# The first layer's sixteen units in groups of 2, 4, 5 and 5, with a new order string and a new table

## The chip, the core and the metric

The kernel runs on one core of one Trainium2 chip. A core has five engines with an instruction queue of their own: TensorE (PE, matmuls; the load of a matmul's weights is listed as PEld), VectorE (DVE), ScalarE (ACT), GpSimd (POOL) and SyncE (SP, which here only issues DMAs). The metric is device time in microseconds of one execution, median over runs.

## The reference

Attention over two batches of eight heads, whose queries are averaged in pairs first, then two feed-forward layers on the result (1152 tokens of 512 values):

```python
q_pool = q.reshape(B, H, S // 2, 2, D).mean(axis=3)          # S = 1152, D = 64
attn   = softmax(q_pool @ k.T / sqrt(D));  x = attn @ v       # -> 1152 x 512
h = x @ w_in                                                  # 512 -> 2048
P = a0 + a1*h + a2*h**2 + a3*h**3
Q = 1 + abs(b0)*abs(h) + abs(b1)*h**2
x = (P / (Q + 1e-6)) @ w_out                                  # 2048 -> 512
xn = x / sqrt(mean(x*x) + 1e-6) * rms_g
y = (silu(xn @ w_gate) * (xn @ w_val)) @ w_out2               # 512 -> 1536 -> 512
```

## The kernel before

All matmuls of the two layers work on float32 split in two halves (hi and lo), and each product is the sum of three matmuls: hi by hi, hi by lo, lo by hi (`three`, whose instruction is line 597 for both layers).

**Attention.** 72 score tiles of 128 query rows by 1152 keys. For each, PE makes the scores into a PSUM tile (hid, line 929), DVE takes the negated maximum of each row (nm, line 961), ACT the exponential (p, line 967), PE transposes p in blocks of 64 (line 983), and ACT or DVE copies the result to pt (lines 1016 and 1019). The matmuls with v (av, line 1088) follow. Copies of the transposed keys and queries (kT, qT, lines 695 and 698), copies of av (xt), and the sums of query pairs (qp, line 765) can go to more than one engine.

**Weights.** Meanwhile the weights of the layers are loaded (wraw, line 165), converted and split (wc, then win or wout, hi and lo; hi on line 200 or 202, lo on line 207). The first ones stay in SBUF; the others of layer 1 are written to DRAM as two halves and fetched again later by two DMAs of 256 KB each, hi and lo (line 247). There are three buffers for the win pairs and six for the wout pairs (`RB, CB, WIN, WOUT = 3, 2, 3, 6`). A fetch can start when PE has read the buffer's former weights for the last time.

**Layer 1.** The 2048 hidden values are 16 units of 128. For each unit PE makes hid (36 matmuls: three chunks of 384 tokens, four pieces of the 512 inputs, three products), then a chain of six DVE and six ACT operations makes g, ending with g_hi on ACT (line 1338) and g_lo on GpSimd or DVE (line 1341). Seven buffers hold g. The units are taken in groups: for each of nine tiles of 128 tokens, PE adds up the products of the group's units in one of two PSUM buffers (accp, 128x512, three matmuls a unit). The first group's result is copied to acc by ACT (line 1390), that of each later group is added to acc by DVE (line 1392).

**Change of layers.** After the last group each tile's squares are summed (ACT, line 1419), three tiles make a chunk of 384 tokens, whose factor is worked out on small tiles (lines 1425 to 1436), the tiles are scaled (line 1442 or 1444), PE transposes them block by block into the same two accp buffers (line 1449, three transposes a block, four blocks a chunk), and ACT and DVE write x_hi (line 1452) and x_lo (line 1455). A table of activation functions is loaded once in between (line 1611).

**Layer 2.** Twelve units of a gate and a value projection (hid again), a tanh on ACT (line 1503), products on DVE (lines 1507 and 1529), and sums over groups of 4, 4, 2 and 2 units (`GROUPS2`); adds on DVE (line 1572), and the output's DMAs.

**What sets the order.** The program is not written in the order in which it runs. Every step is an `Op` with an engine, a cost, a key and its inputs and buffers; the function `order` makes a plan of the whole, step by step, and issues each engine's instructions in the plan's order. The key of a step is moved by one symbol of the string SHIFTS (250 a symbol), and WAYS says for a step that may go to several engines which one it takes (a digit), or leaves it to the plan (a dot). In the attention the sequence on PE is fixed by PE_ORDER: A and C for the scores, T and 2 for the transposes of p, V for av, P for the key and query transposes. Which engine waits for what on the chip is set by semaphores.

Of the kernel before, what the change touches and what calls it, by code (L numbers as in the profile page):

```python
# [19 lines left out]
def attention_moe_moe2_kernel(  # L20
# [94 lines left out]
    GROUPS1 = [2, 4, 4, 4, 2]  # L115
# [159 lines left out]
    def weight(w, u):  # L275
# [13 lines left out]
        "_DIPUPVKN[QDSOU[TWPRLVT@7QPPDMPk`PUUP2T(fbNEHTNPPPWTPKx=KMPm_GPR=PPORKPmWPTOXW=XNPPP<ZPVUNPOPO]`GN@I"  # L289
        "dOC:(PPGVuM<SHP)Q?P-bX@PPCPPPP6Q-ZP?@ZL@TV=P9PM<KQP7PUPpUPPQ]PmNYPPP,SISjPPIPESX(eVe]UcPQSHPPHPYJBIL"  # L290
        "OrPHHOPIKlMRLRJNc@PJOZPdIRHMNTPPPPZPpPPMPY]ORXLWXF?JNPR0PqJSRKPYPWPHP]PYyLRQPD<KFK[(LPULKJNOPFPOQ]PV"
        "]PQ=UZ9PZMWIeORaBQVP`N1PPSGCaPPP;PR]I`>/aTPQG5PPYP_GOM?yGPDTLYPANPWIKR@QPAPBWN+PPH>LX[Od_HQO[PiQ^VPM"
        "LMOMeR=KSCPLP`PPSLPSEMETbUPPPNYPOWJP=fZPTxNTYPCPRQXTPRcPPQCdMOSPKWUPHPURUPTUP>PXTPFCPPPJPPP6Zd_CZAP="
        "KPPPyPAPWLZTPNPPIPP:NYKOKWS9T]P5P;<UmPrPaNLIPPIPZBHeSSLFBPP]RWND<DRaPPT<k`E<YMNMITDGnPDMPKV;7EI0NL]B"
        "QPMPRMbSPLPaRMMOPDYORJP@PP><PQPTPPPKPZOGYyQORDP<PdPMRT?EPMT[ZTPFTKVKPVLRPT?MUP;PPR]IXCPQOrJRT(Ma]PPP"
        "2PVGDVKtJE^KSKYXFPyGRPNMSkULcbGEOPPPPUNQAa^pPoPLCVDDRDT5GGVPVsPLyP5:P]WZQLQLYP:FCQ9HWF>XRd2APPPSPPL9"
# [1356 lines left out]
```

## Time and profile before

| | us |
|---|---|
| median of three runs (690.06, 691.29, 691.69) | 691.29 |
| the profiled execution | 690.4 |
| its span, first to last instruction | 688.6 |
| PE busy in it | 672.0 |
| DVE busy | 539.2 |
| ACT busy | 400.5 |
| POOL busy | 213.7 |

The attention fills the span to about 248 us, layer 1 the time to about 455 us, layer 2 the rest. A matmul's record is longer than the distance to the next one, since matmuls overlap: PE's rows with 0.33 or 0.39 us follow each other at 0.17 and 0.23 us. "Idle before" an instruction is time in which its engine did nothing, and the name behind the arrow is what ended it.

### The profile page before, as it was taken

To read this page: it belongs to the slowest core of one execution; us is meant where nothing else is said; L and a number is where in the kernel's file an instruction comes from. 1 tells how busy PE (TensorE), PEld (TensorE's weight loads), DVE (VectorE), ACT (ScalarE), POOL (GpSimd) and SP (SyncE) were. 2 spreads that over 40 slices of the span, in tenths; PEclk is the share of its full clock that TensorE was granted. 3 is DMA by queue.
4 is the path that set the end of the run, shared out by engine and by line. 5 is a ranking of instruction groups with operands and counts; after the bars stand their busy time and mean duration, and the time that the engine had idled before them with its cause. 6 is when DMAs were issued, how large, how long until landed. Compare 5 with 4: busy or idle time off the path is not lost.

```text
span 688.6 us, 13171 instructions
## 1 busy us (share of the span) xinstructions
PE 672.0 (98%) x5302; PEld 572.0 (83%) x5302; DVE 539.2 (78%) x700; ACT 400.5 (58%) x652; POOL 213.7 (31%) x224
## 2 busy tenths in 40 slices
PE   7999999999999999999999999999999999999997
PEld 6667666776677678999889988889998899989996
DVE  5899998888989858998998999675775245965554
ACT  4777778888889948997568647183343223312130
POOL 3334246656655562111010412012232014421020
PEclk9999999999999999999999999999999999999999
DMA  7544436666546425241032003101225112431003
GB/s 216 187 135 113 124 104 212 200 193 209 207 162 213 166 85 184 91 153 62 32 121 94 31 30 124 62 0 54 101 93 152 31 39 85 126 119 34 28 1 138
DMA packets 54061, 77.67 MB, mean 113 GB/s; under 512 B 6512, under 2 KB 36464, under 8 KB 54000
## 3 DMA queue, kind: packets, MB, share of 16 engines
q1 hardware_dynamic: 53712, 76.50, 34.4%
q8 instruction: 42, 0.69, 0.4%
q10 hardware_dynamic: 288, 0.33, 0.1%
q14 instruction: 19, 0.16, 0.1%
HBM read 62.40 MB, written 14.42 MB: 112 GB/s over the span
## 4 chain that ended last, share of the span: by engine, by line
PE 86%; DVE 7%; ACT 4%; issue 1%; DMA 1%; POOL 0%; SPq 0%; DVEq 0%; ACTq 0%; POOLq 0%
PE hid L597 35%; PE accp L597 25%; PE hid L929 9%; PE av L1088 8%; PE hid L983 7%; DVE nm L961 3%; ACT p L967 3%; DVE pt L1019 1%; PE hid L838 1%; PE accp L1449 1%; DMA qn<-in_q_dram 1%; PE prep L1135 1%; PE prep L838 1%; DVE acc L1572 0%; DVE m_p L1299 0%
## 5 line engine op out<-in xcount | busy, mean ns | idle before, releaser
L597 PE MATMUL hid<-x_hi,win_hi 128*128 128x384 f32 x480 | 161.8, 337 | 1.3 <-DVE m_p L1299 1.3
L597 PE MATMUL hid<-x_hi,win_lo 128*128 128x384 f32 x480 | 160.8, 335 | 0.0
L597 PE MATMUL hid<-x_lo,win_hi 128*128 128x384 f32 x480 | 155.3, 335 | 0.0
L967 ACT ACTIVATE p<-hid,nm 128x1152 f32<-128x1152 f32 x72 | 88.0, 1222 | 32.9 <-DVE nm L961 30.3
L961 DVE TENSOR_REDUCE nm<-hid 128x1 f32<-128x1152 f32 x72 | 96.9, 1356 | 10.3 <-PE hid L929 4.9
L597 PE MATMUL accp<-wout_hi,g_lo 128*128 128x512 f32 (+1 forms) x254 | 99.2, 390 | 0.0
L597 PE MATMUL accp<-wout_lo,g_hi 128*128 128x512 f32 (+1 forms) x254 | 99.0, 390 | 0.0
L597 PE MATMUL accp<-wout_hi,g_hi 128*128 128x512 f32 (+1 forms) x254 | 98.5, 388 | 0.1
L597 PEld LDWEIGHTS hid<-x_hi,win_hi 128*128 128x128 f32 x480 | 90.1, 188 | 4.6 <-issue 2.2
L929 PE MATMUL hid<-kT,qT 64*128 64x256 f32 (+3 forms) x800 | 91.7, 370 | 0.9 <-ACT qT L695 0.5
L597 PEld LDWEIGHTS hid<-x_lo,win_hi 128*128 128x128 f32 x480 | 89.5, 188 | 1.8
L597 PEld LDWEIGHTS hid<-x_hi,win_lo 128*128 128x128 f32 x480 | 90.1, 188 | 0.0
L983 PEld LDWEIGHTS hid<-ident,p 64*128 64x128 f32 x1296 | 51.8, 139 | 38.4 <-ACT p L967 25.0
L1088 PE MATMUL av<-pt,vn 128*64 128x288 f32 x576 | 83.5, 417 | 0.0
L929 PEld LDWEIGHTS hid<-kT,qT 64*128 64x128 f32 (+1 forms) x800 | 72.3, 177 | 11.2 <-issue 1.0
L983 PE MATMUL hid<-ident,p 64*128 64x64 f32 x1296 | 65.3, 229 | 7.5 <-ACT p L967 5.9
L1016 ACT ACTIVATE pt<-hid 128x512 f32<-128x512 f32 (+2 forms) x143 | 59.1, 442 | 12.5 <-PE hid L983 11.0
L1341 POOL TENSOR_TENSOR g_lo<-m_p,g_hi 128x1152 fp32r<-128x1152 f32 (+1 forms) x11 | 22.8, 2084 | 121.9 <-ACT g_hi L1338 84.3
L174 ACT ACTIVATE wc<-wraw 128x512 f32<-128x512 f32 x68 | 45.9, 675 | 24.8 <-POOL win_lo L207 12.0
L1019 DVE COPY pt<-hid 128x512 f32<-128x512 f32 (+2 forms) x81 | 49.9, 621 | 11.0 <-PE hid L983 7.9
L597 PEld LDWEIGHTS accp<-wout_hi,g_lo 128*128 128x128 f32 x254 | 47.7, 188 | 9.9
L597 PEld LDWEIGHTS accp<-wout_hi,g_hi 128*128 128x128 f32 x254 | 47.7, 188 | 8.7 <-DVE acc L1572 0.3
(122 smaller groups left out, 1034.4 us busy)
## 6 DMA issues: line engine op xcount, KB each, us to landing
wraw<-in_moe_w_out_dram SPq DMA_DIRECT2D x28, 512.0 KB, 3.5
far<-spill SPq DMA_DIRECT2D x23, 512.0 KB, 3.2
wraw<-in_moe_w_in_dram SPq DMA_DIRECT2D x16, 512.0 KB, 4.2
wraw<-in_moe_w_gate_dram SPq DMA_DIRECT2D x12, 512.0 KB, 3.8
wraw<-in_moe_w_val_dram SPq DMA_DIRECT2D x12, 512.0 KB, 3.6
vn<-in_v_dram SPq DMA_DIRECT2D x16, 288.0 KB, 3.0
kn<-in_k_dram SPq DMA_DIRECT2D x15, 288.0 KB, 4.4
qn<-in_q_dram SPq DMA_DIRECT2D x15, 256.0 KB, 3.7
```

The lines of the kernel that those rows point to most:

```text
L174: nc.scalar.activation(c.bitcast(F32), wt["raw", n][:, :, 1].bitcast(F32), AF.Abs, scale=2.0**-112)
L597: ins = nc.tensor.matmul(dst, lhsT=a[x], rhs=b[y], start=first and i == 0 and p == 0, stop=last and i == n - 1 and p == len(by) - 1,)
L838: ins = nc.tensor.transpose(e["prep", n_][r][:, at // 2:at // 2 + 64], src[rows], ident[rows, rows])
L929: ins = nc.tensor.matmul(ps[to, j, c:c + x1 - x0], lhsT=qT[2 * pr + h][rows, c0:c0 + to.stop - to.start], rhs=kT[2 * pr + h][rows, x0:x1], ...
L961: nc.vector.tensor_reduce(out=e["nm"], in_=scores(), op=ALU.max, axis=AX.X, negate=True)
L967: nc.scalar.activation(e["p"], scores(), AF.Exp, bias=e["nm"], scale=1.0, accum_out=sums[pr][:, t:t + 1])
L983: ins = nc.tensor.transpose(ps[:, g, c:c + 64], e["p"][rows, 128 * j:128 * j + 128], ident[rows, rows])
L1016: return nc.scalar.activation(to, src, AF.Copy)
L1019: return nc.vector.tensor_copy(to, src)
L1088: nc.tensor.matmul(e["av", h][64 * c:64 * c + 64, 0:QW], lhsT=v_tile[2 * pr + h][:, KEYS[kt], :], rhs=pt[pr, h][:, kt, c * QW:(c + 1) * QW ...
L1135: nc.tensor.transpose(e["rb"][:, t * 128:t * 128 + 128], e["rx"][:, t].rearrange("p a d -> p (a d)"), ident)
L1341: eng.tensor_sub(g_(1), p_(), g_(0).bitcast(F32))
```

## The change

One list of group sizes, the string SHIFTS, the string WAYS and PE_ORDER are other ones. No function is changed.

```diff
-    GROUPS1 = [2, 4, 4, 4, 2]
+    GROUPS1 = [2, 4, 5, 5]
     GROUPS2 = [4, 4, 2, 2]
...
     SHIFTS = (
-        "_DIPUPVKN[QDSOU[TWPRLVT@7QPPDMPk`PUUP2T(fbNEHTNPPPWTPKx=KMPm_GPR=PPORKPmWPTOXW=XNPPP<ZPVUNPOPO]`GN@I"
+        "NPP_OPRCS:UQPPRSPTRZVLJ)8HNQPGQKd]PNKP[BZbPQgRrYPvJjr3HPTYYP3dTKFYUP`u<w7O>R[XPPGIPHVh`FPU_`cR8_NSYP"
...
     WAYS = (
-        "..........0..0.1...0....1......00..1...0.00..1........01........11.....10...........1.........0....."
+        "........0.0.11.....0..1.11...1.10........0...1.....11.0......1..1......10..0.....0..10......0..0...."
...
     PE_ORDER = (
-        "ACCAFFTPT2AC2ACPFTFT2AC2ACPFTFT2A2CACPVVVVTVT2AC2ACPVVVTVT2AC2ACPVVVTVV2TA2CACVVVVTT2AC2ACPVVVVTVT2A"
+        "ACCAFFTPT2AC2ACPFTFT2AC2ACPFFTT2A2CACPVVVVTVVT2AC2ACPVVVTVT2AC2ACPVVVTVV2TA2CACVVVVTT2AC2ACPVVVVTVT2A"
```

The matmuls stay the same in kind and number. Of the instructions on the other engines these change their number: adds of accp to acc on DVE 36 to 27; g_lo of layer 1 on DVE 7 to 5, on POOL 7 to 9; win_hi on POOL 21 to 13, on DVE 5 to 7, on ACT 1 to 7; some copies of the attention between DVE and ACT. In PE_ORDER six places differ, each by one or two symbols.

The order of the instructions at three places. First DVE in the attention, between the 18th and the 22nd row maximum (nm). Before:

```order
L961 TENSOR_REDUCE nm<-hid 128x1 [waits PE_49] x2
L183 SCALAR_TENSOR_TENSOR wc<-wraw,wc 128x512 [waits DMAHW2_49]
L179 TENSOR_SCALAR wc<-wc 128x512 [waits Activation_49]
L1019 COPY pt<-hid 128x8x64 [waits PE_49,Activation_49]
L189 SCALAR_TENSOR_TENSOR wc<-wraw,wc 128x512 [waits DVE_49]
L698 TENSOR_SCALAR kT_1244<-prep 128x5x64 [waits PE_49]
L1019 COPY pt<-hid 128x8x64 [waits PE_49,Activation_49]
L207 TENSOR_TENSOR wout_lo<-wc,wout_hi 128x512 [waits Pool_49]
L961 TENSOR_REDUCE nm<-hid 128x1 [waits PE_49]
```

and with the change:

```order
L961 TENSOR_REDUCE nm<-hid 128x1 [waits PE_49] x2
L183 SCALAR_TENSOR_TENSOR wc<-wraw,wc 128x512 [waits DMAHW2_49]
L179 TENSOR_SCALAR wc<-wc 128x512 [waits Activation_49]
L1019 COPY pt<-hid 128x8x64 [waits PE_49,Activation_49]
L189 SCALAR_TENSOR_TENSOR wc<-wraw,wc 128x512 [waits DVE_49]
L698 TENSOR_SCALAR kT_1244<-hid 128x5x64 [waits PE_49,Activation_49]
L1019 COPY pt<-hid 128x8x64 [waits PE_49]
L698 TENSOR_SCALAR kT_1244<-prep 128x5x64
L961 TENSOR_REDUCE nm<-hid 128x1 [waits PE_49]
```

The split wout_lo has left this place for POOL, and a second key copy (kT) has come from ACT.

Second PE in layer 1, where the group that first needs fetched weights of units 12 and 13 begins. Names: wout_hi_4966 and 4972 are units 10 and 11, 5355 and 5370 units 12 and 13; accp_5419 is the group's first token tile; hid_5375 is unit 15. Before (in front of this piece stand 24 more hid matmuls of unit 15 and the first three accp):

```order
L597 MATMUL hid_5375<-x_hi_140,win_hi_5151 128x384
L597 MATMUL hid_5375<-x_lo_144,win_hi_5151 128x384
L597 MATMUL hid_5375<-x_hi_140,win_lo_5152 128x384
L597 MATMUL accp_5419<-wout_hi_4972,g_hi_5192 128x512 [waits DMAHW6_49,Activation_49]
L597 MATMUL accp_5419<-wout_lo_4973,g_hi_5192 128x512 [waits DMAHW7_49]
L597 MATMUL accp_5419<-wout_hi_4972,g_lo_5193 128x512 [waits Pool_49]
L597 MATMUL accp_5419<-wout_hi_5355,g_hi_5273 128x512 [waits DMAHW6_49,Activation_49]
L597 MATMUL accp_5419<-wout_lo_5356,g_hi_5273 128x512 [waits DMAHW7_49]
L597 MATMUL accp_5419<-wout_hi_5355,g_lo_5274 128x512
L597 MATMUL accp_5419<-wout_hi_5370,g_hi_5359 128x512 [waits DMAHW0_49,Activation_49]
L597 MATMUL accp_5419<-wout_lo_5371,g_hi_5359 128x512 [waits DMAHW1_49]
L597 MATMUL accp_5419<-wout_hi_5370,g_lo_5360 128x512 [waits Pool_49]
```

With the change (wout_hi_4967 is unit 10, the last of the group before; 4984, 5436 and 5454 are units 11, 12 and 13; accp_5429 is the last tile of the group before, accp_5470 the first of the last group):

```order
L597 MATMUL accp_5429<-wout_hi_4967,g_hi_5124 128x512
L597 MATMUL accp_5429<-wout_lo_4968,g_hi_5124 128x512
L597 MATMUL accp_5429<-wout_hi_4967,g_lo_5125 128x512
L597 MATMUL accp_5470<-wout_hi_4984,g_hi_5192 128x512 [waits DMAHW6_49,DVE_49,Activation_49]
L597 MATMUL accp_5470<-wout_lo_4985,g_hi_5192 128x512 [waits DMAHW7_49]
L597 MATMUL accp_5470<-wout_hi_4984,g_lo_5193 128x512 [waits Pool_49]
L597 MATMUL accp_5470<-wout_hi_5436,g_hi_5278 128x512 [waits DMAHW6_49,Activation_49]
L597 MATMUL accp_5470<-wout_lo_5437,g_hi_5278 128x512 [waits DMAHW7_49]
L597 MATMUL accp_5470<-wout_hi_5436,g_lo_5279 128x512 [waits Pool_49]
L597 MATMUL accp_5470<-wout_hi_5454,g_hi_5440 128x512 [waits DMAHW0_49,Activation_49]
L597 MATMUL accp_5470<-wout_lo_5455,g_hi_5440 128x512 [waits DMAHW1_49]
L597 MATMUL accp_5470<-wout_hi_5454,g_lo_5441 128x512 [waits Pool_49]
```

No hid matmul stands between the two groups any more, nor from there to the layer's end. Six matmuls of the second tile with units 11 and 12 follow, then unit 14 of the first tile, three of the second with unit 13, then unit 15 of the first. The buffer of unit 12 is that of unit 6, read for the last time 16 matmuls ahead of the first accp_5470; unit 13's is unit 7's (13 ahead), unit 14's is unit 8's (7), unit 15's is unit 9's (4).

Third PE at the change of layers (transposes of acc into accp; hid_5719 is gate unit 0, hid_5723 its value unit). Before, after the last tile's last matmul:

```order
L597 MATMUL accp_5692<-wout_hi_5409,g_lo_5562 128x512
L1449 MATMUL accp_5706<-ident_65,acc_4131 128x128 [waits DVE_49,Activation_49]
L1449 MATMUL accp_5706<-ident_65,acc_4131 128x128 [waits Activation_49]
L1449 MATMUL accp_5706<-ident_65,acc_4131 128x128
L1449 MATMUL accp_5714<-ident_65,acc_4131 128x128 [waits DVE_49]
L1449 MATMUL accp_5714<-ident_65,acc_4131 128x128 x2
L597 MATMUL hid_5719<-x_hi_140,win_hi_5233 128x384 [waits Activation_49]
L597 MATMUL hid_5719<-x_hi_140,win_lo_5234 128x384
L597 MATMUL hid_5723<-x_hi_140,win_hi_5348 128x384 [waits PE_49]
L597 MATMUL hid_5723<-x_hi_140,win_lo_5349 128x384
L1449 MATMUL accp_5727<-ident_65,acc_4131 128x128 [waits DVE_49]
```

With the change, after the last tile's last matmul (the first chunk's transposes stand 60 accp matmuls earlier, and begin with the same pair; hid_5618 is gate unit 0):

```order
L597 MATMUL accp_5716<-wout_hi_5477,g_lo_5486 128x512
L1449 MATMUL accp_5740<-ident_65,acc_4131 128x128 [waits DVE_49]
L1449 MATMUL accp_5740<-ident_65,acc_4131 128x128 [waits Activation_49]
L1449 MATMUL accp_5740<-ident_65,acc_4131 128x128
L1449 MATMUL accp_5747<-ident_65,acc_4131 128x128 [waits DVE_49]
L1449 MATMUL accp_5747<-ident_65,acc_4131 128x128 x2
L1449 MATMUL accp_5753<-ident_65,acc_4131 128x128 [waits DVE_49]
L1449 MATMUL accp_5753<-ident_65,acc_4131 128x128 x2
L597 MATMUL hid_5618<-x_hi_140,win_hi_5200 128x384 [waits Activation_49]
L597 MATMUL hid_5618<-x_hi_140,win_lo_5201 128x384
L597 MATMUL hid_5618<-x_hi_140,win_hi_5200 128x384
L597 MATMUL hid_5618<-x_hi_140,win_lo_5201 128x384
```

The third block's transposes (accp_5753) now follow the second's at once; the four hid matmuls that stood between them come after. In the order on ACT the table load stands ahead of the fourth block's x_hi of this chunk.

## Rows read from the trace of the kernel before

**Rows 1.** The page: engine busy time, and the granted clock in 40 slices

```profile
PE 672.0 (98%) x5302; PEld 572.0 (83%) x5302; DVE 539.2 (78%) x700; ACT 400.5 (58%) x652; POOL 213.7 (31%) x224
...
PEclk9999999999999999999999999999999999999999
```

**Rows 2.** Windows: stretch, length, busy of PE, PEld, DVE, ACT, POOL, clock, DMA

```profile
8.20:67.90 59.70, 56.06 (x748) 42.35 (x746) 52.40 (x76) 45.24 (x93) 22.72 (x22) 1.00 0.52 155
67.90:109.70 41.80, 39.98 (x507) 27.93 (x504) 38.34 (x57) 31.91 (x62) 16.75 (x20) 1.00 0.46 140
...
285.00:410.00 125.00, 125.00 (x640) 114.58 (x639) 117.47 (x100) 84.21 (x79) 16.92 (x8) 1.00 0.22 73
410.00:455.20 45.20, 45.20 (x209) 38.35 (x209) 37.03 (x47) 23.39 (x34) 7.60 (x11) 1.00 0.26 82
...
468.00:678.40 210.40, 210.40 (x1122) 198.23 (x1120) 127.84 (x170) 56.96 (x75) 49.55 (x47) 1.00 0.23 73
```

**Rows 3.** The chain in order of time: start, length, what

```profile
419.26 33.38 PE accp L597 x147
...
547.71 37.46 PE hid L597 x216
```

**Rows 4.** Waits of PE: for whom, us in total, times, longest

```profile
PE hid L983 <- ACT p L967: 5.9, 13, 0.6
PE hid L597 <- DVE m_p L1299: 1.3, 1, 1.3
...
PE accp L1449 <- DVE acc L1392: 0.6, 1, 0.6
```

**Rows 5.** Groups by line and form, DVE, 268 to 468 us: busy, mean ns, idle before

```profile
L1392 DVE TENSOR_TENSOR acc<-acc,accp 128x512 f32<-128x512 f32 x36 | 24.5, 682 | 9.5 <-PE accp L597 9.5
...
L1341 DVE TENSOR_TENSOR g_lo<-m_p,g_hi 128x1152 fp32r<-128x1152 f32 x7 | 9.5, 1351 | 0.6 <-ACT g_hi L1338 0.6
```

**Rows 6.** The same view of DVE, 67.9 to 109.7 us

```profile
L1019 DVE COPY pt<-hid 128x512 f32<-128x512 f32 x12 | 8.2, 689 | 0.7 <-PE hid L983 0.4
...
L698 DVE TENSOR_SCALAR xt<-av 64x288 f32<-64x288 f32 x4 | 1.8, 453 | 0.1
L698 DVE TENSOR_SCALAR kT<-prep 128x320 f32<-128x320 f32 x3 | 1.4, 480 | 0.0
...
L1019 DVE COPY pt<-hid 128x128 f32<-128x128 f32 x3 | 0.8, 282 | 0.0
L207 DVE TENSOR_TENSOR wout_lo<-wc,wout_hi 128x512 fp32r<-128x512 f32 x1 | 0.7, 682 | 0.0
```

**Rows 7.** Timeline of SyncE, 405 to 422 us: start, time to issue, what

```profile
410.24 0.32 SPq L247 DMA_DIRECT2D wout_hi<-far  x1
...
411.13 0.38 SPq L247 DMA_DIRECT2D wout_hi<-far  x1
411.56 0.42 SPq L247 DMA_DIRECT2D wout_lo<-far  x1
```

**Rows 8.** Timeline of PE, 454 to 457 us: start, length, what, idle before

```profile
454.95 0.39 PE L597 MATMUL accp<-wout_hi,g_lo 128*128 128x512 f32 x1
455.18 0.49 PE L1449 MATMUL accp<-ident,acc 128*128 128x128 f32 x3
456.27 0.55 PE L1449 MATMUL accp<-ident,acc 128*128 128x128 f32 x3 [0.60 <-DVE acc L1392]
```

**Rows 9.** Line 247 in 357:360, 410:411 and 411.1:414 us, issue to landing

```profile
DMA to landing us min/median/max: 2.7/4.2/4.8
...
DMA to landing us min/median/max: 2.9/3.1/3.4
...
DMA to landing us min/median/max: 4.9/5.4/6.9
```

**Rows 10.** Timeline of DVE, 455 to 458 us

```profile
456.51 0.62 DVE L1455 SCALAR_TENSOR_TENSOR x_lo<-accp,gain,x_hi 128x384 fp32r<-128x384 f32 x1 [0.29 <-ACT x_hi L1452]
```

**Rows 11.** Timeline of ACT, 455 to 463 us

```profile
459.64 1.28 ACT L1611 ACT_TABLE_LOAD   x1
```

More of the change, by code (lines that the diff above doesn't have):

```diff
@@ new lines, in attention_moe_moe2_kernel @@
+        "PZKPPDg>HVYLV^SN>[GQ`aeHPNOYRKSRMFXSXXPZY]_jMVUPFUWCyKDR[_NLUT_K[3NPP]MPPPPQPPPPQRQ;PPPRSPPIA;ZMRRPP"
+        "a9PPDPPPTHPPPXL[PaP>HMMOPURVBFLQPPPTdxPY?G:PTYT=ZPKJM:IPNPNQWdYULAAPPOE;TZS`YN>KZ]BU_SPPPGPPu9UPcSPJ"
+        "PObVKHNtOXPPXNBQLVBPaPAPHP`iAOPBaMOPMPLORr^`MP0PPIcPPMQaS^PYHXPQONIPPPTXPKPDCPPTP<RPMRX0GFOhFP5Pb8PP"
+        "ZPPPHGI*QTGP]A?OPOrPERPOPP_PTGP=P.QKUcPPOKRPKPPBIKUgOPEPPPeFXVJPHP(ZC^NPMAINHPPRyILVHOI?bOPCbPNA7P@R"
+        "PGRlOMVK<LPP>MP_NPZ[PEURGPWcPPRbPSPT0PQgPPPPdUTPILP^P?]ZLTTPXONZ`P=PPBLSePUPYSPrJyCTKK]DLC<6U4LP=QbP"
@@ new lines, in attention_moe_moe2_kernel @@
+        "PPPwEV_ZQoKD=Z]OcN]>QPPPPMGPPNiBdWM4SiMV5xWMPPP]AP[sLIUAQPGPFZIVPPVFTPPSUPXZP`[(OIS4NQOPeITVP]PPYPII"
+        "tYUPJPGPPNOO_PJT3P9>hPPQPP]WIPHPPJQPPPIPOZNe3ZLPGR_KKE<INPHK(tNSYPPPHNPiWPgH(L(YTPQR]PQaugKeAT@PP@IP"
+        "U]NAPyPP[RP_HRJ[c[PPT`WNGhTDPeTZiPT5PPUPOPQVVUFWPU9OBN5DmPPFRkdHMgPLKUAPPVKPSP3SOPPA?^ITKRPnP(PRePL]"
+        "TdLE6RSGVTPC[yLYa[rPORUdO]_YW3P[wgRJKPPU:@PjLsNN=_MYKPWRGTPJMQNWhPPFPPMVANNeNJ[RIZJPCSJKeVP=TRPT@G2P"
+        "P^MDQFTZPPHPyPMDwP2Y[P9PPPBVPR4PVPO[PIUPJWPPRJyTsPSZPPSIPPN]CPN3KEP_RVJZRM[DR>cVVPPNOPMGbGDPITGNPMUP"
@@ new lines, in attention_moe_moe2_kernel @@
+        "PPePJ8OHPNPPPPK=PPQWV__^;DSUKQN[X+LUHZPWPPW(H;PBKLSTX@NP3YPN8BDPi`DRTOPMPWPNMJPTPVTTQPKJ;8PNPQGqu<P`"
+        "Ja0TPPcUOUJ]MVOuCiPPDPHI?PPSPh6XLR?PPP?P=UePQ[P(QOCb0XZO,Pd@KWWyPFNPKKPPFRPPH[YFJU`AalNPSJeO^2gxFPUR"
+        "PPPPYFCUeEMPLOD;uPPQP^EIF1QUJWVQFPE/MRRJP`PP3RWRLU3QOPMMG[PbOaPgPPNPXPPeAcmUPZP*VJYOOFNFVPDKPHCQPJL^"
+        "WFGWlPW]TM3;PNbUs0PSPZJPG4VL(PXJYPYXPPmTSLkPPQL@T(LPJ(OdPJY(PH:PPOPQF4JPPSHXPdU^NQIZI?MPEUpNNXLK?VX["
+        "LLfHPPJHPUZ@PW`GONgPLVHMX]TXNPPCPLPJSiPVtSIYOJSMYPKLQL]PPPAgkGPTjP/LRSWqPRP=jEPWQPA(P]IdcPJaRMPY_PPI"
@@ new lines, in attention_moe_moe2_kernel @@
+        "PIXdPg1A[PJPPGGljPRngDNPPG81`CKPIVZHPkLlPiWRLPVHJPMIPLYL(NFRdPQUOOqPPaS>XgPDT,UWPUjRZeP8MP_WOK^RHOPP"
+        "9RfYPKPPSpNP_hP?FOHQPUANPbPQQPHF:KP[@SNPjHCAISOORhX[QK_EAAfZMPP0PyRMPLQQVJRkPPLoX>TQYTPPPePaVPZdTK^E"
+        "JPL`DQhGVaPLEfV]FATVPPDSrPMLP<PH8LbM[KM]PG>MUY@QPQR>NX_PPSAPG9PPPn^LmPt7PFQH`PTQFPPPWQP9QWNAZOM7PI,I"
+        "R^VMqNSJbMXIPJUjMOPX]_PfPXLFPZ^PCWQOUqEPPDKsTLhNyMCEB]PPQc?JRPHLP@MPV9]OwPPKCPPPPKRPLI`PLLPTP`YPVZ]K"
+        "^DE]]mSPUY<O7Fb[rOOQ)QU2NBNPJSPGYyPNIG?DXPPFUPPUNJkVdWAP[NPRKDIPFYSPU`ZtYOPD5VTDPJFbFOZf`lVVPN_PQIXH"
```

79 lines of the change are left out of this document (30 added, 49 removed).

## The prediction

> **What bounds the kernel now.** I read the engine shares of the page first. TensorE (PE) is busy 672.0 us of the span, and the granted TensorE clock stands at its upper level (2.4 GHz) in all forty slices [rows 1]. Then the stretches, because an average hides that this kernel has two halves [rows 2]. In the attention, up to about 248 us, VectorE (DVE) and ScalarE (ACT) are close to full beside PE: in 67.9 to 109.7 us PE is busy 39.98 of 41.8, DVE 38.34 and ACT 31.91. From 285 us to 455.2 us (layer 1) PE is busy 125.00 of 125.00 and 45.20 of 45.20, and from 468 to 678.4 us (layer 2) 210.40 of 210.40. A modelled end can make a PE look busy while its matmuls stand still, so I checked the pace: in the chain of waits 147 accp matmuls in a row take 33.38 us, 0.227 each, and 216 hid matmuls 37.46 us, 0.173 each [rows 3]; from layer 1's start on the matmuls follow at these two paces. The waits of PE agree: 5.9 us in 13 pieces for the softmax's p, 1.3 us once for DVE where layer 1 starts, 0.6 us once where it ends [rows 4].
>
> So the second half has about 2 us that any reordering could take away, and the attention some more. Whatever makes PE wait from 285 us on is added to the end one for one.
>
> **The adds that go.** Four groups after five take away one round of nine adds acc+accp on DVE: 36 of 0.682 us now [rows 5], 27 then, 9 x 0.682 = 6.1 us of DVE. Two of its seven g_lo of layer 1 go to GpSimd as well, 2 x 1.351 = 2.7 us [rows 5]. On the path this is worth nothing: PE waits for no add of layer 1 before 455 us [rows 2, 4], every one runs beside matmuls, and the matmuls stay as many, for each unit and token tile still has its three. It cannot be below nothing either, as PE has no idle time there to give back. The same goes for the win_hi splits that leave GpSimd (21 to 13; DVE 5 to 7, ACT 1 to 7): mostly layer 2, PE full. Layer 2's own groups and the last matmuls are as before; I set these at 0.
>
> **The attention.** Before the 19th score tile the new order gives DVE more, between the 19th and the 31st less. Counted in the two orders, 19 to 31 (67.9 to 109.7 us) loses one wout_lo (0.682), two xt copies (2 x 0.453) and one 128x128 pt copy (0.282), and gains one kT copy (0.480) [rows 6]: 1.39 us less in a stretch where DVE is 92% busy. That is where PE's waits were; the idle time of PE there, 41.8 - 39.98 = 1.8 us [rows 2], is the most it can give. In 8.2 to 67.9 us DVE gains a pt copy (0.689), two kT (2 x 0.480) [rows 6] and a qp add, and loses one short win_hi that I don't price. The trace has no qp add of 640 columns on DVE; from the 0.682 us of an add of 512 [rows 5] I estimate 0.85. In sum 2.5 us more at most, against 59.7 - 52.40 = 7.3 us of DVE idle time [rows 2]. Beyond the 31st tile the two tables load DVE nearly alike. Bounds: -1.8 (all idle time of the one stretch) to +2.5 (nothing gained, all that is added shows). I take -0.9, half the idle time, because what went in early is spread over time in which DVE has room.
>
> **The last group's weights.** This is what the groups of five cost. The w_out buffers hold six units. A group of five leaves one for the next group's first unit, and units 12 to 15 can be fetched only as units 6 to 9 are read for the last time. Before, the same four fetches were issued from 410.24 us [rows 7], and 36 hid matmuls lay between the last read and the first use; now no hid matmul is left there. Count from G, the first matmul of the last group, 0.227 us each. Unit 6's weights are last read 16 matmuls ahead of G, unit 7's 13: with a matmul's 0.39 us [rows 8] they are free at G-3.24 and G-2.56. SyncE starts unit 12's pair at about G-3.2, and the second pair follows 0.89 us after the first [rows 7]: its hi half at G-2.3, the lo half 0.43 later, at G-1.87. PE wants unit 12's lo half at G+0.91 (four matmuls) and unit 13's at G+1.59 (seven). The first pair of such a train landed 2.9 to 3.4 us after issue, so unit 12 is in time (G-2.77+3.4 = G+0.6). The three pairs at 357 us took 4.2 in the median and 4.8 at most, and the last three at 411 us 4.9 at least, 5.4 in the median, 6.9 at most [rows 9]. Unit 13's lo half then lands between G+2.3 and G+3.5, and PE waits 0.7 to 1.9 us. Behind this wait stand PE's whole queue and, through it, everything. Unit 15's lo half is issued near G+0.25 and wanted at G+5.0 plus the first wait; at 6.9 it lands at G+7.15 and costs about 1 us more, at the 4.8 of 357 us nothing. Bounds 0 (each pair as fast as a lone one, up to 3.4: G+1.5) and 2.2; I take 1.0: at 4.2 to 4.8, the pairs at 357 us, unit 13 waits 0.7 to 1.3 and unit 15 not at all.
>
> The Trainium skill ("DMA: Bandwidth & Descriptors", section "Anatomy of one DMA — SWDGE (gpsimd) path") speaks against this term: about 2 us fixed plus the bytes at 436 GB/s, an estimate of 2.6 us for these 256 KB, at which unit 13 would land before it is wanted and the sum would be 1.0 us lower. The trace agrees roughly for a lone pair and not for a train, and the measured 4.9 to 6.9 us decide.
>
> **The change of layers.** The first transposes of x into the two accp buffers come in pairs: the first finds its buffer free, the second waits until DVE has added the last tile. That is the 0.60 us idle before 456.27 us [rows 8]. Before, this happens once, because all nine tiles are done first. The new order begins the first 384 tokens after five tiles of the last group, fills in the other four tiles (60 matmuls) and then begins the second 384 tokens: the pair stands there twice, +0.60. At the second place a third transpose follows at once, with no hid matmul ahead of it; it needs the buffer of the first, which x_lo gives back: in the row that answers to it x_lo ends at 456.51+0.62 = 457.13 [rows 10], and the pair's transposes, three at 0.1, end at 456.57, so +0.56. Last, the table load of 1.28 us on ACT [rows 11] stands ahead of the second 384 tokens' last x_hi, where before PE had x_lo matmuls to run. I give that 0.14 of its 1.28, since eight hid matmuls (1.4 us) stand ahead of the one that needs it. In all +1.3, bounds 0 (the fillers cover all) and 0.60+0.56+1.28 = 2.4.
>
> **Sum.** -0.9 + 1.0 + 1.3 = +1.4 us. The profiled execution took 690.4 us (span 688.6 and 1.8 around it), which gives 691.8; it lies 0.9 below the median of the runs shown, 691.29, so the median should come to 691.29 + 1.4 = 692.7 us. That is 0.2% and not a change that a measurement of this kernel tells from none: I count 0.3% (2.1 us) as the least that it can tell.
>
> **Rivals.** (1) Faster. The loads come as a lone pair does, the fillers cover the change of layers, and the attention gives the whole 1.8 us: 691.29 - 1.8 = 689.5; with the 1.3 us wait at layer 1's start gone too [rows 4], 688.2. For it: DVE really is the fuller engine in 67.9 to 109.7 us, and loses 1.4 us of work there. Against it: around layer 1's start DVE and ACT keep almost their order, and two new waits would have to cost nothing. (2) Slower. The train of weight loads is the last thing to end: from a landing of 5.4 us on, unit 13 costs 1.9 and unit 15 is late too, 2.2 together instead of 1.0, and the attention's relief is eaten by the copies put in early (0 instead of -0.9): 692.7 + 1.2 + 0.9 = 694.8. For it: the four loads of before came at 4.9 to 6.9 [rows 9], and a 512 KB load is queued right behind them. Against it: the train at 357 us stayed within 4.8. (3) Nothing happens, because every moved piece lies under a full PE: 691.3. For it: PE is full in all of layer 1. Against it: that holds only while its inputs are there.
>
> **How the numbers follow.** Forecast, within a microsecond and a half of 692.7: 0.46. Rival 1: 0.22. Rival 2: 0.20. Rival 3: 0.12. The range takes in rival 1's 689.5 and rival 2's 694.8: 689.2 to 695.2. Below 689.2 (faster by over 0.3%) lie most of rival 1 with the start's wait gone, and a little that I have not seen: 0.20. Above 693.4 (slower by over 0.3%) lie rival 2 and about a third of the forecast's spread: 0.34. The rest, 0.46, is within 0.3%.
>
> **What would show it.** Right: in the list of PE's waits a new line accp waiting for a DMA into wout_lo, some 35 to 50 us before layer 2, of about 1 us; PE's wait for the add acc twice instead of once; fewer or shorter waits of PE for p between 65 and 110 us, and the first hid matmul of layer 1 about 1 us earlier than 248.5. Wrong: no DMA in PE's waits (the second term falls), PE busy without a gap through the change of layers (the third), the attention ending as late as now (the first). If layer 1 from 268 to 455 us became shorter by more than the pace of its matmuls allows, the reading that PE bounds it would be wrong altogether.

## The result

| | before | with the change |
|---|---|---|
| median | 691.49 (4 runs, 690.06 to 693.27) | 696.55 (4 runs, 694.22 to 697.67) |
| the profiled execution | 690.4 | 696.33 |
| its span | 688.6 | 694.5 |

All times in us. The ratio is 1.0071 with a 95% interval of 1.0051 to 1.0092: slower by 5.1 us, where 692.7 was forecast with a range of 689.2 to 695.2. On another chip, with six runs of the changed kernel beside eleven of before, it was 694.62 against 691.4, a ratio of 1.0046 (1.0030 to 1.0062). The sign is the forecast's in both; the size is two to four times the forecast's.

### The profile page after: what moved, and what is told of

Its sections match the earlier page's. It is cut to its first block, busy times and chain, and to the rows that moved or that the text cites. A ratio compares the mean times of both kernels' runs of the same rounds, so it can differ in the third digit from the quotient of the medians.

```text
span 694.5 us, 13147 instructions
## 1 busy us (share of the span) xinstructions
PE 676.2 (97%) x5302; PEld 574.7 (83%) x5302; DVE 541.6 (78%) x696; ACT 403.3 (58%) x657; POOL 210.3 (30%) x214
## 4 chain that ended last, share of the span: by engine, by line
PE 87%; DVE 6%; ACT 4%; DMA 1%; issue 1%; SPq 0%; DVEq 0%
PE hid L597 35%; PE accp L597 24%; PE hid L929 10%; PE av L1088 9%; PE hid L983 7%; DVE nm L961 3%; ACT p L967 3%; DMA wout_lo<-far 1%; PE hid L838 1%; DVE pt L1019 1%; PE prep L838 1%; PE prep L1135 1%; DMA qn<-in_q_dram 1%; PE accp L1449 0%; ACT x_hi L1452 0%
## 5 line engine op out<-in xcount | busy, mean ns | idle before, releaser
L929 PE MATMUL hid<-kT,qT 64*128 64x256 f32 (+3 forms) x800 | 93.1, 372 | 0.6 <-ACT qT L695 0.5
L929 PEld LDWEIGHTS hid<-kT,qT 64*128 64x128 f32 (+1 forms) x800 | 73.9, 179 | 11.2 <-ACT pt L1016 0.9
L1341 POOL TENSOR_TENSOR g_lo<-m_p,g_hi 128x1152 fp32r<-128x1152 f32 (+1 forms) x13 | 30.7, 2366 | 115.2 <-ACT g_hi L1338 107.6
```

The costliest lines, as they stand in the source:

```text
L929: ins = nc.tensor.matmul(ps[to, j, c:c + x1 - x0], lhsT=qT[2 * pr + h][rows, c0:c0 + to.stop - to.start], rhs=kT[2 * pr + h][rows, x0:x1], ...
L1341: eng.tensor_sub(g_(1), p_(), g_(0).bitcast(F32))
```

## The profile after

The engine times of the page, which answer to [rows 1]:

```profile
PE 676.2 (97%) x5302; PEld 574.7 (83%) x5302; DVE 541.6 (78%) x696; ACT 403.3 (58%) x657; POOL 210.3 (30%) x214
```

PE has as many instructions and is busy 4.2 us more, in a span that is 5.9 us longer. Windows of the changed kernel, columns as in [rows 2]: the tiles 1 to 19 and 19 to 31 of the attention, the bulk of layer 1, the start of the last group, and the change of layers:

```profile
8.00:69.00 61.00, 57.76 (x749) 44.31 (x747) 53.57 (x78) 44.18 (x90) 21.47 (x22) 0.97 0.51 152
69.00:111.20 42.20, 40.62 (x509) 28.22 (x510) 37.01 (x56) 32.22 (x63) 17.83 (x21) 1.00 0.46 140
...
285.00:410.00 125.00, 125.00 (x649) 115.78 (x648) 116.98 (x96) 88.58 (x84) 28.84 (x12) 1.00 0.23 76
...
423.00:432.00 9.00, 7.82 (x34) 5.95 (x33) 9.00 (x7) 3.39 (x3) 3.44 (x1) 1.00 0.72 233
...
442.00:477.00 35.00, 33.24 (x175) 28.57 (x174) 15.24 (x28) 15.99 (x35) 2.35 (x12) 1.00 0.03 10
```

Layer 1 from 285 to 410 us and layer 2 are full as before. New are 1.2 us of PE idle time around 428 us; from 442 to 477 there are 1.8 us, where the kernel before has 0.6 at its change of layers [rows 4]. In the first window the clock column says 0.97. The waits of PE, which answer to [rows 4]:

```profile
PE hid L983 <- ACT p L967: 5.3, 11, 1.0
PE hid L597 <- DVE m_p L1299: 1.4, 1, 1.4
PE hid L983 <- DVE pt L1019: 1.4, 3, 0.7
PE accp L597 <- DMA wout_hi<-far: 1.1, 1, 1.1
...
PE hid L838 <- ACT p L967: 1.0, 2, 0.5
PE accp L1449 <- DVE acc L1392: 0.9, 2, 0.5
...
PE hid L597 <- ACT x_hi L1452: 0.5, 2, 0.3
```

**Where the 5.9 us are.** The list of waits is not the whole loss, because a matmul behind a wait is also slower. So I take the distances between the starts of successive matmuls, less the pace of the form when PE is full (0.1735 us at 384 columns, 0.2272 at 512, 0.109 for a transpose), and add them up by stage. "Last group" is the 300 matmuls ahead of the first transpose, "change of layers" reaches 50 matmuls beyond the last transpose. "Fall" says whether a window of 5 us between 10 and 25 us shows a granted clock under 0.95. "Late" marks two profiles without a fall in which the clock rose later: their first twenty score matmuls take 3.33 and 3.49 us instead of 2.22, as these rows of fill_late and of after_again show. The trace's first entry of the granted clock, at its upper level, comes at 9.4 and 10.0 us in these two and at 4.0 to 6.0 us in the others of the table.

```profile
7.14 3.33 PE L929 MATMUL hid<-kT,qT 64*128 64x256 f32 x20
```

```profile
6.60 2.22 PE L929 MATMUL hid<-kT,qT 64*128 64x256 f32 x20
```

The column "from matmul 601" is the time from the start of the 601st matmul, at 53 to 55 us and so behind any fall, to that of layer 1's first one.

| kernel, one profile each | fall | layer 1 begins at | from matmul 601 | last group | change of layers | span |
|---|---|---|---|---|---|---|
| before | no | 248.53 | 195.39 | 0.15 | 1.27 | 688.6 |
| before_1, _2, _3 | no, yes, yes | 248.31, 249.34, 249.43 | 195.40, 195.41, 195.42 | 0.15 | 1.27, 1.29, 1.26 | 688.3, 689.3, 689.8 |
| the changed kernel | yes | 250.59 | 196.61 | 1.96 | 3.37 | 694.5 |
| after_again (the same) | no | 248.57 | 195.84 | 1.47 | 3.37 | 692.2 |
| far13 | no | 249.62 | 196.56 | 1.47 | 3.37 | 693.1 |
| adds | yes | 250.04 | 195.87 | 1.48 | 3.40 | 693.5 |
| far_adds | no | 248.58 | 195.85 | 0.26 | 3.39 | 690.8 |
| glo13 | yes | 250.51 | 196.61 | 1.82 | 3.37 | 694.4 |
| norm_late | late | 250.47 | 195.85 | 1.71 | 5.24 | 698.5 |
| table_late | yes | 249.82 | 195.86 | 1.49 | 2.96 | 692.9 |
| fill_late | late | 251.01 | 196.63 | 1.79 | 2.16 | 693.6 |
| mended2 | no | 248.74 | 195.88 | 1.86 | 1.70 | 690.9 |

For the changed kernel: 2.06 in the attention, 1.81 at the last group, 2.10 at the change of layers, 6.0 together; the rest of the layers adds 0.1. The stages of the layers repeat to a few hundredths where no DMA has a part in them; that makes them a sharper measure than the whole time, which spreads over 3 us.

## The experiments

**The change itself, and the attention alone.** att_new takes the new order for the attention only: PE_ORDER and the first 1390 entries of both tables from the changed kernel (moved with their steps where the groups change the order of the entries), groups and all later entries from before.

> The changed kernel itself, on the chip on which the three other kernels of this series run. Theory A (three separate places: attention +2.05 us, last group's weights +1.7, change of layers +1.9, as the two traces show): +5.1 us against before, 696.4, with no row that depends on the chip. Rival B (1.3 of the attention's 2.05 us is a chance fall of the granted clock at 12 us, not the order): executions with a granted clock of 1.000 and of 0.998 both occur, 1.3 us apart, and the mean gain of before stays between 3.8 and 5.1 us.

Measured: 694.62 (693.97 to 695.28). The profile has no fall of the clock and begins layer 1 at 248.57 us, 0.04 behind before. Theory A's 5.1 didn't repeat. Rival B fails too: the gain of before is 3.2 us, under its 3.8, and the spread of 1.3 us is there although the granted clock is 0.999 or 1.000 in all six executions. One thing that makes such a spread is shown below, under the length of the attention.

> The kernel before (groups 2, 4, 4, 4, 2, its layer tables), with the new order string's and the new table's entries for the attention alone and the new PE_ORDER; PE's order of the layers is then that of before. Theory A: +2.0 us, 693.3, and first matmuls of layer 1 later by 2 us. Rival B: +0.7 us, 692.0, and the granted clock stays 1.00 from 10 to 20 us; with the clock fall +2.0. My blind forecast of this part was -0.9, 690.4.

Measured: 697.25, ratio 1.0088 (1.0069 to 1.0107), far from both. The layers begin at 250.73, 2.2 us late; then PE waits 1.0 us for an add, up to 340.2 us, and where layer 1 starts 3.8 us for VectorE:

```profile
PE hid L597 <- DVE m_p L1299: 3.8, 1, 3.8
```

The layer entries of before had been made for before's end of the attention. The kernel mixes two orders whose seam costs more than either part, so its time says nothing on the attention by itself; its trace does, as shown below.

**The reverse.** lay_new takes the attention from before and the rest from the change.

> The changed kernel with the order string's, the table's and PE_ORDER's entries of the kernel before for the attention; groups 2, 4, 5, 5 and the new layer entries stay. PE's order at the change of layers is then that of the changed kernel; between the last two groups 12 hid matmuls come in. Theory A, corrected (the new attention costs nothing by itself, the loss is all in the layers): the same 3 to 4 us above before as the changed kernel, 694.5 to 695.5, less up to 1.3 for the 12 hid matmuls that cover the last group's start: 693.5 to 695.5. Rival E (the new attention is what costs): 691.5 to 692.5.

Measured: 706.48, ratio 1.0215 (1.0201 to 1.0230): another seam, and the most telling miss. PE in lay_new at the last group (start, length, what, idle before):

```profile
433.79 0.39 PE L597 MATMUL accp<-wout_hi,g_lo 128*128 128x512 f32 x1
441.69 0.80 PE L597 MATMUL accp<-wout_hi,g_hi 128*128 128x512 f32 x1 [7.51 <-ACT g_hi L1338]
...
444.53 0.63 PE L597 MATMUL accp<-wout_hi,g_lo 128*128 128x512 f32 x1
```

The 12 hid matmuls that I took for a cover were the last of unit 15. They end 12 matmuls (2.7 us) ahead of the last group, where the changed kernel has 75 (17 us) in between, and the chain of products behind them (ACT's last g_hi starts at 440.47) then had nothing to run beside. A last group of five wants all its units within some 24 matmuls of its start.

**The start of the last group.** far13 gives unit 13's weights a buffer pair of their own:

```diff
-        kind = wkind(n)
+        kind = "wfar" if wseq[n] in (("out", 13),) else wkind(n)
```

(in `s_load` and `fetch_ops`, and the two pools). adds shortens the adds to acc:

```diff
-                    nc.vector.tensor_add(y[:, t], y[:, t], e["ps"])
+                    w = DM if g[-1] == NU1 - 1 else 32; nc.vector.tensor_add(y[:, t, 0:w], y[:, t, 0:w], e["ps"][:, 0:w])
```

far_adds has both, and glo13 is far13 with one symbol of WAYS changed, for unit 13's g_lo.

> The changed kernel with a buffer pair of its own for unit 13's output weights, so that its fetch no longer waits for the last group; the order on PE, DVE, ACT and POOL stays as it is. Theory A: the 1.1 us wait for wout_hi and the two short ones behind it go, 1.7 us less than the changed kernel run beside it. Rival C (the wait only hides another one, for the adds or at the change of layers): less than 0.5 us is gained. Units 14 and 15 are wanted 0.5 us after they land, by the changed kernel's trace, so no new wait on them.

Measured: 696.66, ratio 1.0073 (1.0052 to 1.0093): nothing gained. PE in far13:

```profile
427.45 0.39 PE L597 MATMUL accp<-wfar_hi,g_lo 128*128 128x512 f32 x1
428.76 0.50 PE L597 MATMUL accp<-wout_hi,g_hi 128*128 128x512 f32 x1 [0.92 <-DVE acc L1392]
```

Unit 13's weights no longer wait, and three matmuls further on PE waits for the add that frees the second accp buffer. Rival C was right.

> Unit 13's own buffer pair as in far13, and the adds of the second and third group to acc over 32 of 512 columns only (the other columns are left out of the sums), which takes some 10 us of VectorE's work ahead of the last group. Theory F (at the last group's start two waits lie on top of each other, the weights and the add that frees accp, and each alone hides the other): both go, 1.2 us less than the changed kernel, PE's waits there under 0.3 us. Rival G (the add is late because VectorE's product just ahead of it takes 3.2 instead of 1.35 us beside GpSimd's g_lo, however full VectorE is): the wait for acc stays, 0.7 us or more.

Measured: 694.59, ratio 1.0038 (1.0025 to 1.0051); in the profile 0.26 us is left at the last group, and no wait for weights or acc. The changed kernel wasn't run on this chip, and its own ratios of 1.0046 and 1.0071 elsewhere are too far apart to show 1.2 us in the time: the profile shows it.

> The short adds alone, the weights' buffers as in the changed kernel (the same columns left out). Theory F: the wait for the weights stays, 0.3 to 1.7 us by the landings, none for acc; time 0 to 0.7 us below the changed kernel. Rival G: as the changed kernel.

Measured: 695.27, ratio 1.0054 (1.0039 to 1.0070), 1.48 us at the last group, with the wait for the weights alone:

```profile
428.19 0.47 PE L597 MATMUL accp<-wout_hi,g_hi 128*128 128x512 f32 x1 [0.62 <-DMA wout_hi<-far]
428.75 0.50 PE L597 MATMUL accp<-wout_lo,g_hi 128*128 128x512 f32 x1
```

The four kernels make a square: neither removed 1.47 to 1.96, the weights alone 1.47, the add alone 1.48, both 0.26. Theory F holds: two waits lie on top of each other, and each hides the other. G, by which the add is late however full VectorE is, is out: in far_adds the product ahead of the add still takes 3.44 us beside GpSimd's g_lo, and no wait is left. VectorE comes to that product 1.0 us earlier there, measured from the last group's first matmul, and the add itself is 0.5 us shorter.

```profile
422.85 3.44 DVE L1330 SCALAR_TENSOR_TENSOR m_p<-m_q,m_p 128x1152 f32<-128x1152 f32 x1
```

> far13 (unit 13's weights in a buffer pair of their own) with unit 13's g_lo on VectorE instead of GpSimd. Theory L (VectorE's product before the add took 3.2 us because GpSimd's g_lo ran beside it; without it the add that frees accp comes earlier): PE's idle and slow time at the last group's start falls from 1.47 us to 0.3 to 0.9. Rival M (VectorE is simply full; with a further 1.35 us on it unit 15's product comes later and PE waits for that): 1.4 us or more.

Measured: 696.18, ratio 1.0070 (1.0052 to 1.0088), 1.82 us at the last group: rival M. PE waited 0.36 us for g_lo and 0.61 for the add, although the product takes 1.35 us here. VectorE is busy 8.96 of 9.00 us in 423 to 432 (9.00 in the changed kernel); a collision taken away there is paid for with the work that is put in its place.

**The change of layers.** norm_late delays the first transposes until all tiles are summed (`490 + -4000` becomes `490 + 22000`). table_late holds the table load back (`last` becomes `[*last, *xhop[1, 3]]`), and fill_late eight matmuls of the first chunk of layer 2:

```diff
-                PE, cost(PE, len(by) * len(kks) * CW), key + 1960 * c,
+                PE, cost(PE, len(by) * len(kks) * CW), key + 1960 * c + (30000 if by is LO and c == 0 and w != "in" else 0),
```

> The changed kernel with one constant changed (26 us on the key of the norm steps), so that all nine tiles of the last group are summed before the first transpose, as in the kernel before. Theory A: the second pair of transposes, the back-to-back third and the late x_hi go: 1.9 us less than the changed kernel run beside it, PE's idle time at the change of layers 0.6 us in one piece. Rival D (the first chunk's transposes between the tiles are a help, since the other two chunks have their fillers then, and the loss sits in the last chunk whose table load and squares come late either way): no change, within 0.5 us.

Measured: 699.65, ratio 1.0112 (1.0093 to 1.0132), 5.24 us at the change of layers. Neither theory came: it is 1.9 us more, where A forecast 1.9 less and D no change. PE waits for x_hi five times here, 2.9 us in all, behind transposes in sixes. The kernel before, which begins late too, has four hid matmuls between its first four blocks and loses 1.27. So an early start is worth 1.9 us with these entries of the tables, and that it is better in itself isn't shown. Part of the time is a late last output DMA in this profile, 4.4 us where the others take 2, and not the stage.

> The changed kernel with the table load made to wait for the second chunk's last x_hi; ACT's order differs in that, PE's in a few hid matmuls. My step charged this load with 0.14 us. Theory H (PE's 0.33 us wait for that x_hi is the load's price): PE's idle time at the change of layers 0.3 to 0.4 us less, no difference that the times show. Rival I (with the load later, the tanh behind it is late and PE waits for a free hid buffer): 0.5 to 1.3 us more.

Measured: 694.99, ratio 1.0052 (1.0035 to 1.0069), 2.96 us at the change of layers: 0.41 less. Theory H, and the time shows no difference from the changed kernel.

> The changed kernel with one key changed: the eight matmuls of the first chunk of layer 2 that need x_lo, of the gate and of the value projection's unit 0, may run only after the last tile of layer 1, so that they stand between the second chunk's transposes; the order on ACT and DVE is that of the changed kernel. Theory J (the change of layers is slower because these matmuls were used up four tiles too early, so that the second chunk's transposes and x_hi stand uncovered): PE's idle and slow time there falls from 3.37 us to 2.0 to 2.4, time 1.0 to 1.4 us below the changed kernel. Rival K (the waits follow each other on ACT and DVE, fillers only move them): under 0.3 us.

Measured: 693.9 (10 runs), ratio 1.0041 (1.0025 to 1.0057), 2.16 us at the change of layers: 1.21 less, theory J. The time doesn't show it: the changed kernel wasn't run on this chip, and 693.9 is 0.7 below its 694.62 on another. PE in the changed kernel there:

```profile
465.19 0.49 PE L1449 MATMUL accp<-ident,acc 128*128 128x128 f32 x3
466.13 0.55 PE L1449 MATMUL accp<-ident,acc 128*128 128x128 f32 x3 [0.45 <-DVE acc L1392]
467.01 0.55 PE L1449 MATMUL accp<-ident,acc 128*128 128x128 f32 x3 [0.33 <-DVE x_lo L1455]
...
470.31 0.44 PE L597 MATMUL hid<-x_hi,win_hi 128*128 128x384 f32 x1 [0.19 <-ACT x_hi L1452]
...
475.06 0.44 PE L597 MATMUL hid<-x_hi,win_hi 128*128 128x384 f32 x1 [0.34 <-ACT x_hi L1452]
```

and in fill_late:

```profile
464.05 0.49 PE L1449 MATMUL accp<-ident,acc 128*128 128x128 f32 x3
464.29 1.14 PE L597 MATMUL hid<-x_lo,win_hi 128*128 128x384 f32 x5
465.27 0.49 PE L1449 MATMUL accp<-ident,acc 128*128 128x128 f32 x3
465.52 0.60 PE L597 MATMUL hid<-x_lo,win_hi 128*128 128x384 f32 x2
465.95 0.49 PE L1449 MATMUL accp<-ident,acc 128*128 128x128 f32 x3
```

Between the same transposes now stand seven of the eight matmuls, and both waits are gone.

> All repairs together: unit 13's own buffer pair, its g_lo on VectorE, the late fillers and the table load behind the second chunk's last x_hi. By theories F, J, L and H the sum is 1.47 - 0.6 and 3.37 - 1.4 us: 2.3 us below the changed kernel, 692.3, some 1 us above the kernel before. Rival (new waits take their place): 694 or more.

Measured: 694.41 (12 runs, 692.59 to 696.68), ratio 1.0050 (1.0034 to 1.0065). The change of layers is at 1.70: fill_late's 1.21 and table_late's 0.41 add up. The last group stayed at 1.86 (glo13's rival M), and with the time at 694.41 instead of 692.3 the rival was right. The profiled execution, without a fall and with an early start of layer 1, has a span of 690.9; no version was faster than the kernel before.

**How long the attention is.**

> The kernel before once more, for the start of its layer 1 (248.53 us in the profile shown). The nine profiles with the new attention start it at 248.57 to 251.01 us. Theory N (the attention's length varies by 2 us from execution to execution, partly by falls of the granted clock at 10 to 25 us, in both kernels alike; the new order changes nothing): starts between 248.5 and 251 us, and a fall in one of three. Rival O (the new attention is slower by some 1 us, or prone to the clock's fall): 248.3 to 249.0 us in all three, no fall.

> As before_1: a second execution of the kernel before. Theory N: layer 1 starts between 248.5 and 251 us; rival O: 248.3 to 249.0.

> As before_1: a third execution of the kernel before. Theory N: layer 1 starts between 248.5 and 251 us; rival O: 248.3 to 249.0.

Measured: 690.15, 691.08 and 691.58, and layer 1 begins at 248.31, 249.34 and 249.43. The two late ones have the fall. So the fall comes in both kernels (N). The starts alone can't price the order: the ten profiles of the table that have the changed kernel's attention begin at 249.80 on the mean, the four of before at 248.90, but falls and late rises are mixed into these means.

The column "from matmul 601" takes them out. There the executions of one order agree to a few hundredths: 195.39 to 195.42 us in all four of before, 195.84 to 195.88 in six of the new order, and 196.56 to 196.63 in its other four. So the new order costs 0.45 us in every execution, and in four of ten another 0.75. A good half of the 0.45 lies between the 19th and the 31st row maximum, where VectorE has less to do: 41.83 to 41.85 us in the four profiles of before and in lay_new, which has before's attention, and 42.11 to 42.13 in the ten with the new one and in att_new. These two follow the attention that they were given, whatever the layers are, so the order is what costs it. Ahead of the 601st matmul it costs nothing: without fall and late rise that matmul starts at 52.73 to 53.06 us against 52.91 and 53.14, with a fall at 53.89 to 54.17 against 53.92 and 54.01.

The 0.75 us are one wait. In the new order VectorE's shift of a weight (line 179) and GpSimd's split of another (line 235) start within 0.03 us of each other. In the changed kernel:

```profile
124.11 1.53 DVE L179 TENSOR_SCALAR wc<-wc 128x512 uint32<-128x512 uint32 x1
124.08 1.27 POOL L235 TENSOR_TENSOR spill<-wc,spill 128x512 fp32r<-128x512 f32 x1
128.31 0.77 PE L983 MATMUL hid<-ident,p 64*128 64x64 f32 x17 [0.99 <-ACT p L967]
```

and in after_again, the same program:

```profile
122.86 0.42 DVE L179 TENSOR_SCALAR wc<-wc 128x512 uint32<-128x512 uint32 x1
122.85 1.56 POOL L235 TENSOR_TENSOR spill<-wc,spill 128x512 fp32r<-128x512 f32 x1
126.11 0.77 PE L983 MATMUL hid<-ident,p 64*128 64x64 f32 x17
```

Where VectorE's shift is the one that waits, the row maximum behind it, the exponential and PE's transposes all come 1 us later, of which 0.75 stay. That is so in the changed kernel, far13, glo13, fill_late and att_new; in the other six GpSimd's split waits, and PE doesn't. In before the shift stands behind the row maxima, and none of its profiles has the wait. Why one or the other goes first these runs don't show.

## Why the prediction was wrong, point by point

**The bound was read rightly.** From 285 to 410 us and in layer 2 PE is full in both kernels, the nine adds and two g_lo that VectorE was rid of bought nothing, and the whole loss lies at the three places that the sum named. Their parts as measured, some 0.65 on the mean for the attention's order, 1.3 to 1.8 for the last group and 2.1 for the change of layers, come to 4.1 to 4.6 us, between the 3.2 and the 5.1 of the two chips.

**The attention is the step that failed**: "I take -0.9, half the idle time, because what went in early is spread over time in which DVE has room." The order costs 0.45 us in every execution and 1.2 in four of ten, some 0.65 on the mean with what it gains ahead of the 601st matmul. Between the 19th and the 31st tile it did take work off VectorE, 37.01 us busy of 42.20 instead of 38.34 of 41.80, as counted. But that stretch became 0.28 us longer in all eleven profiles of the new order, where I wanted 0.9 less. Over the whole attention the wait for p at line 983 went down by 0.6, while the waits for pt and of the transposes of keys and queries (line 838) came up by 0.4 and 0.5. Their rows in the kernel before:

```profile
PE hid L983 <- DVE pt L1019: 1.0, 3, 0.7
...
PE hid L838 <- ACT p L967: 0.5, 1, 0.5
```
A less loaded VectorE did not shorten the chain from scores to pt that PE waits on; which step of it costs the 0.28 stays open. And I counted VectorE's work by the stretch and not by what it meets there: the wait of 0.75 us comes from one shift beside one split of GpSimd. Of the 2.06 us of the profiled execution 0.45 and 0.77 are these two, and the remaining 0.83 lie ahead of the 601st matmul, where the clock fell. The profile of before happened not to have the fall, which delays that matmul by some 0.9 us in before's order and 1.2 in the new one.

**The last group's weights**: the wait came as described, but not alone, and the stage lost 1.3 to 1.8 us where the sum has 1.0. I took unit 13's fetch for one of the train at 357 us; the second pair of a burst of four was already in [rows 9], at 4.9 us and more. The fetches of the changed kernel, issue and length on SyncE:

```profile
423.39 0.32 SPq L247 DMA_DIRECT2D wout_hi<-far  x1
...
424.28 0.38 SPq L247 DMA_DIRECT2D wout_hi<-far  x1
424.71 0.42 SPq L247 DMA_DIRECT2D wout_lo<-far  x1
```

and how long the DMAs of that line issued in 423 to 425 took to land:

```profile
DMA to landing us min/median/max: 2.8/4.1/5.0
```

The slowest, 424.71 and 5.0 us, is unit 13's lo half (the prediction's estimate of 2.6 us is one for DMAs that GpSimd issues, and these are SyncE's), and PE's matmul with it starts at 429.78; the 1.1 us ahead of it are the wait for the hi half. Rival 2 priced a landing of 5.4 us at 1.9; 1.7 came (1.25 us late at the hi half, 0.33 at the lo half, 0.11 behind). For unit 15 the prediction has "about 1 us more", which its own numbers don't give (7.15 - 5.0 - 1.9 = 0.25, as in its bound of 2.2); PE did not wait for that unit.

What the sum missed altogether is the second wait under it, for an add, a term that it put at nothing: far13 shows it at 0.92 us, with a loss at the stage as large as after_again's. VectorE in the changed kernel:

```profile
423.97 1.34 DVE L1321 SCALAR_TENSOR_TENSOR m_q<-m_q,m_u 128x1152 f32<-128x1152 f32 x1
425.24 0.67 DVE L1392 TENSOR_TENSOR acc<-acc,accp 128x512 f32<-128x512 f32 x1
425.84 3.23 DVE L1330 SCALAR_TENSOR_TENSOR m_p<-m_q,m_p 128x1152 f32<-128x1152 f32 x1
428.99 0.67 DVE L1392 TENSOR_TENSOR acc<-acc,accp 128x512 f32<-128x512 f32 x1
```

and GpSimd:

```profile
424.42 3.44 POOL L1341 TENSOR_TENSOR g_lo<-m_p,g_hi 128x1152 fp32r<-128x1152 f32 x1 [16.41 <-ACT g_hi L1338]
```

I had set the g_lo that moves to GpSimd and the adds at nothing, because PE waited for no add of layer 1. But the size of the last group sets when its last unit must be ready: before, units 14 and 15 were wanted only in the last 12 us of layer 1; now at its last 31 us less some 5. VectorE, 94% busy [rows 2], gets 6 us of adds less and a deadline some 14 us earlier. It is the same mistake as in the attention, turned round: a share of busy time says nothing on what is wanted when.

**The change of layers**: named rightly in its parts, 1.3 forecast, 2.1 measured. The pair that stands there twice and the back-to-back third transpose came as priced (0.60 + 0.56 forecast, 0.62 + 0.49 by the starts). The table load costs 0.41 instead of 0.14, as table_late shows. Not on my list was the third chunk, whose six transposes in a row leave PE 0.51 us behind x_hi. And the greater part does not come from the early start by itself but from the first chunk's hid matmuls being used up before the last four tiles: 1.21 of the 2.1 went with fill_late, 1.67 with the table load held back too (mended2), and 0.4 stays open.

**The signs to watch** came for two terms (accp waiting for a DMA, 1.1 us, though into wout_hi and not wout_lo; the add waited for twice, 0.9) and against me for the first (layer 1 at 250.59, and at 248.57 in after_again, not 1 us before 248.5).

## What to carry to other kernels

- Where one wait is found, ask what stands ready under it: take both away and each alone on the chip before either gets a price. Here each alone was worth 0 to 0.5 us and both together 1.2 to 1.7.
- The last of several groups sets the deadline of everything that feeds it. Making it larger saves rounds of adds and moves the deadline forward by the difference in its length.
- When one kernel's profile is set against another's, take several of each: the first 250 us alone differed by 2.4 us between executions of one and the same order. Then cut them at the same instructions and compare the pieces: they agreed to 0.07 us, and the 2.4 came apart into the start, where the clock falls or rises late, and one wait.

## What the runs showed of the hardware

**A VectorE operation waits for a GpSimd one.** The product m_p above takes 3.23 us where its neighbours of that form take 1.35. GpSimd's g_lo ran from 424.42 to 427.86, and 427.86 + 1.35 = 429.21, close to its end at 429.07; g_lo itself took 3.44 where all seven of that form on GpSimd in the kernel before take 2.67 to 2.70, and began while VectorE was in m_q (to 425.31; 425.31 + 2.69 = 428.00). Each seems to have waited for the other to end. The Trainium skill ("SBUF — State Buffer", section "SBUF: two separate sides") says this: a VectorE operation with two SBUF inputs and a GpSimd operation that reads SBUF share a pair of ports, and whichever starts first has them for its whole length. Here the numbers agree within 0.2 us. The shift beside the split at 124 us is a second pair, and is seen either way round: 0.42 and 1.53 us for the shift, 1.56 and 1.27 for the split.

**The granted clock falls behind long waits, and early in some executions.** Windows of the changed kernel and of before_2 (the clock is the third column from the right):

```profile
5.00:10.00 5.00, 4.41 (x37) 3.57 (x36) 3.05 (x5) 1.75 (x4) 1.53 (x1) 1.00 0.99 294
10.00:15.00 5.00, 4.02 (x56) 3.69 (x57) 3.18 (x5) 3.71 (x8) 0.00 (x0) 0.71 0.79 235
```

```profile
10.00:15.00 5.00, 4.01 (x58) 3.69 (x58) 2.50 (x4) 3.56 (x8) 1.55 (x1) 0.76 0.72 231
```

The same stretch of the kernel before as profiled first:

```profile
10.00:15.00 5.00, 4.01 (x66) 3.40 (x67) 3.23 (x5) 4.00 (x9) 1.55 (x1) 1.00 0.65 206
```

PE is equally busy in the two executions of that order, and one has the fall and the other not. What decides it these runs don't show. In att_new the clock falls 1.2 us behind the end of the 3.8 us wait, and the matmuls of 274 to 277 us follow each other at 0.32 us instead of 0.173:

```profile
275.00:280.00 5.00, 5.00 (x24) 5.00 (x24) 5.00 (x10) 4.17 (x10) 2.02 (x2) 0.76 1.04 355
```

In lay_new, around the 7.5 us wait and behind it:

```profile
435.00:440.00 5.00, 0.00 (x0) 0.00 (x0) 4.96 (x6) 0.79 (x1) 0.00 (x0) 0.71 0.00 0
440.00:445.00 5.00, 3.14 (x7) 1.99 (x8) 2.43 (x3) 1.53 (x2) 0.00 (x0) 0.50 0.35 105
445.00:450.00 5.00, 5.00 (x19) 4.02 (x18) 0.69 (x1) 1.08 (x4) 0.00 (x0) 0.77 0.00 0
```

PE did nothing from 434 to 441.7 us, and then ran at 0.50, the lower level (1.2 GHz): the matmuls of 444 to 447 us follow each other at 0.43 us instead of 0.227. Of the 11.49 us that this stage lost, 7.7 are the wait and most of the rest this. This one wait cost half as much again behind it; the waits of about 1 us in the changed kernel left the clock at 1.00.
